# A tanh-shrink MLP behind a dynamic convolution: one f tile in halves, and the first x tile loaded body first

## The chip, the cores and the metric

The kernel runs on one core of a Trainium2 chip. Times are device microseconds (us) of one execution. A profile is one further execution, recorded with all engines: PE is the matmul engine (TensorE) and PEld its weight loads, DVE is VectorE, ACT is ScalarE, POOL is GpSimd, SP is SyncE, which issues most of the DMAs. "L257" is line 257 of the kernel before.

## The reference

`x` is 8 x 4096 x 192 in float32, `weight_gen` 8 x 4096 x 8 heads x 7 taps, `moe_w_in` 192 x 2048, `moe_w_out` 2048 x 192. A softmax over the taps gives each position and head seven weights; they weigh the current row and the six rows ahead of it (zeros before the start of a batch). The result goes through a two-layer MLP whose activation is `h - tanh(h)`:

```python
w = exp(weight_gen - max); w = w / (sum(w) + 1e-9)
x_unf = x_pad[:, idx]                      # 7 rows for each position, K = 7
conv = einsum('bshk,bskhg->bshg', w, x_unf)   # 32768 x 192
h = conv @ w_in                            # 32768 x 2048
out = (h - tanh(h)) @ w_out                # 32768 x 192
```

## The kernel before, in words

The 32,768 tokens are cut into 32 superblocks of 1,024 tokens, numbered n; a partition holds J = 8 consecutive tokens. Batch starts are every fourth n, where the six halo rows of partition 0 are zeros.

For each n there are three stages, which run for different n at the same time.

Stage one makes the convolution products. `load_x` (L99) brings x with its halo, 14 rows of 192 for each partition, over SP's queue; `load_wg` (L89) brings the tap weights. `softmax_exp` (L132) is one exponential on ACT, `softmax_norm` (L142) a sum and a reciprocal on DVE. `products` (L169) multiplies x by the weights, one operation for each of the seven taps k, all on POOL except for n = 0 and 1, where DVE takes some (`on_vector`). For n = 0 DVE has taps 3, 4, 5 and 6 and POOL taps 0, 1 and 2. For n above 2 a DMA on POOL's queue adds the odd products to the even ones.

Stage two is `conv` (L217): PE transposes the products and sums them in PSUM by 64x64 matmuls against an identity, and ACT copies the sums to `convT` (L244). From n = 2 on, superblock n + 1 is transposed inside superblock n, after the f tiles 12 and 13: 104 matmuls into two PSUM tiles called `pc`, the first for chunks 0 and 1, the second for chunk 2.

Stage three is the MLP. `gemm1(n, f)` (L252) makes one of 16 f tiles: six matmuls of 512 columns into a PSUM tile `ph` of 128 x 1024 float32 [...], a tanh on ACT into `th` (L267), and the subtraction on DVE into the bf16 tile `gt` (L269). `gemm2` (L276) makes one token block of the second matmul from the 16 `gt` tiles of superblock n - 1, 32 matmuls into `obank`, and ACT copies the result out (L307).

`ph` and `pc` share one rotation of three PSUM buffers (tag "ph", `psum_h` with bufs = 3), so a matmul that opens a new tile waits until the tile three earlier has been read by all its readers. The order of work is written out by hand (`manual_schedule`): each engine runs its instructions in program order. In a superblock n > 1, step p = 0 to 7 is: f tile 2p, f tile 2p + 1, one `gemm2`. At p = 6 the two `conv` calls come after it, and then the sum and reciprocal for superblock n + 3. So around the transposes the tiles take the buffers in this order: f tile 12 the first, f tile 13 the second, `pc` of chunks 0 and 1 the third, `pc` of chunk 2 the first, f tile 14 the second, f tile 15 the third, f tiles 0 and 1 of the next superblock the first and the second.

At the start, SP issues in this order: tap weights of 0, then x of 0 (zero rows, row block 0, partitions 1 to 15, partitions 16 to 127: L117, L121, L107), tap weights of 1, x of 1. POOL first waits for the normalised weights of n = 0 and then issues three DMAs for the first part of `w_in` (columns below `FA` = 8 x 128, L358), and makes its three products; behind tap 2 it issues the rest of `w_in`. Each part of `w_in` is loaded to the lower 64 partitions and then copied to the upper 64 (L369): the first copy is issued on ACT's queue, the second on SP's.

Of the kernel before, what the change touches and what calls it, by code (L numbers as in the profile page):

```python
# [11 lines left out]
ACT = mybir.ActivationFunctionType  # L12
# [4 lines left out]
def kernel(  # L17
# [8 lines left out]
    nc = tc.nc  # L26

    B, S, D = x.shape
    H, K = weight_gen.shape[2], weight_gen.shape[3]
    G = D // H  # L30
    F = moe_w_in.shape[1]
    P = nc.NUM_PARTITIONS
    R = P // 2
    HALO = K - 1

    J = 8
    TOK = P * J
# [3 lines left out]
    NTOT = B * NSB  # L41
    NFT = F // P
    NC = D // R
    GC = G // NC
# [31 lines left out]
    last_act = {}  # L76
    g1_act = {}
    last_sub = {}
    last_wsm = {}

    def order(inst, other, reason):
        tc.add_manual_dep(
            inst.ins,
            other.ins.name,
            mybir.DependencyInfo(mybir.DependencyClass.Sync, mybir.DependencyReason.DATA),
            reason=reason,
        )

    def load_wg(n):  # L89
        b, s = divmod(n, NSB)  # L90
        s0 = s * TOK
        wg_t = wgpool.tile([P, J, H, K], FP32, name="wg_t")
        nc.sync.dma_start(  # L93
            out=wg_t[:],
            in_=weight_gen[b, s0 : s0 + TOK].rearrange("(p j) h k -> p j h k", p=P),
        )
        wg_of[n] = wg_t

    def load_x(n):  # L99
        b, s = divmod(n, NSB)  # L100
        s0 = s * TOK

        x_t = xpool.tile([P, HALO + J, D], FP32, name="x_t")

        def rows(p0, p1):
            win = x[b, s0 + p0 * J - HALO : s0 + p0 * J - HALO + 1]
            nc.sync.dma_start(  # L107
                out=x_t[p0:p1, :, :],
                in_=bass.AP(
                    tensor=win.tensor,  # L110
                    offset=win.offset,
                    ap=[[J * D, p1 - p0], [D, HALO + J], [1, D]],
                ),
            )

        if s == 0:
            nc.sync.dma_start(  # L117
                out=x_t[0:1, 0:HALO, :],
                in_=zero[:].rearrange("o (h d) -> o h d", h=1).to_broadcast([1, HALO, D]),
            )  # L120
            nc.sync.dma_start(  # L121
                out=x_t[0:1, HALO : HALO + J, :],
                in_=x[b, 0:J].rearrange("(p j) d -> p j d", p=1),
            )

            rows(1, 16)
            rows(16, P)
        else:
            rows(0, P)
        x_of[n] = x_t  # L130

    def softmax_exp(n):  # L132
        wg_t = wg_of.pop(n)
        e_t = wgpool.tile([P, J, H, K], FP32, name="e_t")
        nc.scalar.activation(  # L135
            out=e_t[:].rearrange("p j h k -> p (j h k)"),
            in_=wg_t[:].rearrange("p j h k -> p (j h k)"),
            func=ACT.Exp,
        )
        e_of[n] = e_t  # L140
# [21 lines left out]
    def scale(eng, wsm, e_t, zr):  # L162
        return eng.tensor_mul(  # L163
            wsm.rearrange("p j h k -> p (j h) k"),
            e_t[:].rearrange("p j h k -> p (j h) k"),
            zr.rearrange("p (n o) -> p n o", o=1).to_broadcast([P, J * H, K]),
        )

    def products(n, on_vector=(), sums=None, hooks={}, behind=None):  # L169
        x_t = x_of.pop(n)  # L170
        wsm, wsm_v, e_t, zr = wsm_of.pop(n)
        if e_t is not None:
            first = scale(nc.gpsimd, wsm[:], e_t, zr[:])
            if behind is not None:


                order(first, behind, "pace")
        in_pairs = n not in PLAIN

        even = ppool.tile([P, NPAIR, NC, J, H, GC], BF16, name="even")  # L180
        odd = ppool.tile([P, NPAIR, NC, J, H, GC], BF16, name="odd")
        last = ppool.tile([P, NC, J, H, GC], BF16, name="last")
        dst = {}
        for i in range(NPAIR):
            dst[2 * i] = even[:, i]
            dst[2 * i + 1] = odd[:, i]
        dst[K - 1] = last[:]
        if -1 in hooks:
            hooks[-1]()
        for k in range(K):  # L190
            eng, w = (nc.vector, wsm_v) if k in on_vector else (nc.gpsimd, wsm[:])
            eng.tensor_mul(  # L192
                dst[k].rearrange("p c j h g -> p j h c g"),
                x_t[:, k : k + J, :].rearrange("p j (h c g) -> p j h c g", h=H, c=NC),
                w[:, :, :, k : k + 1]
                .rearrange("p j h (k o) -> p j h k o", o=1)
                .to_broadcast([P, J, H, NC, GC]),
            )
            if k == K - 2 and in_pairs:

                nc.gpsimd.dma_start(  # L201
                    out=even[:].rearrange("p i c j h g -> p (i c j h g)")[:, 0:ACC],
                    in_=odd[:].rearrange("p i c j h g -> p (i c j h g)")[:, 0:ACC],
                    accum_op=mybir.AluOpType.add,
                    max_dma_last_dim=4096,
                )
            if k in hooks:
                hooks[k]()
        if in_pairs:
            groups = [even[:, i] for i in range(NPAIR)] + [last[:]]  # L210
            prods_of[n] = [
                groups + ([odd[:, NPAIR - 1]] if c == NC - 1 else []) for c in range(NC)
            ]
        else:
            prods_of[n] = [[dst[k] for k in (sums or range(K))]] * NC
# [33 lines left out]
        if parts[-1][-1] == NC - 1:  # L249
            prods_of.pop(n)  # L250

    def gemm1(n, f):  # L252
        convT = conv_of[n]
        ph = psum_h.tile([P, 2, HT], FP32, name="ph", tag="ph")
        for c in range(NC):
            for r in range(2):
                nc.tensor.matmul(  # L257
                    ph[:, r, :],
                    lhsT=w_in[r * R : (r + 1) * R, c, f * P : (f + 1) * P],
                    rhs=convT[r * R : (r + 1) * R, c, :],  # L260
                    start=(c == 0),
                    stop=(c == NC - 1),
                )
        th = tpool.tile([P, TOK], FP32, name="th")
        ph_f = ph[:].rearrange("p r t -> p (r t)")
        g1_act[0] = last_act.get(0)
        last_act[0] = nc.scalar.activation(out=th[:], in_=ph_f, func=ACT.Tanh)  # L267
        gt = gpool.tile([P, TOK], BF16, name=f"gt{f}", tag=f"gt{f}")
        last_sub[0] = nc.vector.tensor_sub(gt[:], ph_f, th[:])  # L269
        g_of.setdefault(n, []).append(gt)  # L270

    LAST = (NTOT - 1) * J
# [76 lines left out]
    def load_w_out():  # L349
        nc.gpsimd.dma_start(out=w_out[:], in_=moe_w_out.rearrange("(c p) e -> p c e", c=NFT))  # L350

    FA = 8 * P

    def load_w_in(f0, f1):

        for c in range(NC):
            src = moe_w_in[c * GC : c * GC + 1, f0:f1]
            dma = nc.gpsimd.dma_start(  # L358
                out=w_in[0:R, c, f0:f1],
                in_=bass.AP(  # L360
                    tensor=src.tensor, offset=src.offset, ap=[[G * F, H], [F, GC], [1, f1 - f0]]
                ),
            )
            if f0 == 0:

                order(dma, last_wsm[0], "order of the loads")

    def copy_w_in(f0, f1, eng):
        eng.dma_start(out=w_in[R:P, :, f0:f1], in_=w_in[0:R, :, f0:f1])  # L369

    def rest_of_w_in():
        load_w_in(FA, F)

# [4 lines left out]
    load_wg(1)  # L378
    load_x(1)
    load_w_in(0, FA)  # L380
    products(
        0,
        on_vector=(3, 4, 5, 6),
        sums=(3, 0, 4, 5, 1, 6, 2),
        hooks={2: rest_of_w_in},
    )
    softmax_exp(1)
# [1 line left out]
    load_wg(2)  # L389
    copy_w_in(0, FA, nc.scalar)  # L390
    copy_w_in(FA, F, nc.sync)
    products(1, on_vector=(0, 1), hooks={4: load_w_out})
    conv(0, (0, 1), (2,))
    load_x(2)
    for n in range(NTOT):
        if n + 3 < NTOT:
            load_wg(n + 3)
            load_x(n + 3)
        for p in range(J):
            gemm1(n, 2 * p)  # L400
            gemm1(n, 2 * p + 1)
            if n == 0 and p == 1:
                softmax_exp(2)
            if p == 5 and n + 3 < NTOT:
                softmax_exp(n + 3)
            if n >= 1:
                gemm2((n - 1) * J + p)
            if p == 0 and 1 <= n < NTOT - 2:
                products(n + 2, behind=last_sub[0] if n > 1 else None)
            if n + 1 < NTOT:  # L410
                if p == (6 if n > 0 else 7):
                    conv(n + 1, (0, 1))
                if p == (6 if n > 1 else 7):
                    conv(n + 1, (2,))
            if n == 0 and p == 2:
                softmax_norm(2)
                products(2)
            if p == 6 and n + 3 < NTOT:
                softmax_norm(n + 3)
# [33 lines left out]
```

The softmax here doesn't subtract the row's maximum and nothing guards it: scores larger than these inputs give would overflow.

## Time and profile before

| | |
|---|---|
| time, median of 3 runs | 770.32 us (770.04 to 771.87) |
| the profiled execution's own time | 770.86 us |
| its span (first to last instruction) | 768.7 us |
| busy: PE, DVE, ACT, POOL | 96%, 85%, 83%, 90% |
| granted TensorE clock | 1.00 |
| one tanh of 128x1024 (L267) | 1,022 ns, 512 of them |
| one subtraction of 128x1024 (L269) | 1,219 ns, 512 of them |
| one product on POOL (L192) | 2,903 ns |

The profile page has the busy share of each engine, the span in slices, the chain of work that ended last, and groups of instructions by line with the idle time ahead of them and what ended it. The trace behind it can be asked for a timeline of a stretch: the start, the length, engine, line, what is written and read, and how often. Equal instructions that follow each other are merged ("x2"); the length is then that of the whole group. A bracket at the end is the idle time of that engine ahead of the group, and what ended it.

### The profile page before, as it was taken

How to read it: one execution, taken by the hardware profiler on the slowest of the kernel's cores; microseconds unless marked ns; L12 is line 12 of the kernel's file. 1: busy time of each engine (PE TensorE's matmuls, PEld its weight loads, DVE VectorE, ACT ScalarE, POOL GpSimd, SP SyncE). 2: the span in 40 equal slices, each digit the busy share in tenths (PEclk: the TensorE clock that was granted, in tenths of full speed). 3: DMA queues.
4: the chain of work that ended last, by engine and by line, in shares of the span. 5: the costliest groups of instructions: out<-in, count | busy, mean ns of one | idle time of the engine just before them, and what ended most of it. 6: DMA issues, size and time to landing. Idle time of an engine off the chain costs nothing.

```text
span 768.7 us, 32330 instructions
## 1 busy us (share of the span) xinstructions
PE 736.7 (96%) x14784; PEld 583.1 (76%) x14784; DVE 652.9 (85%) x595; ACT 640.8 (83%) x865; POOL 695.2 (90%) x290
## 2 busy tenths in 40 slices
PE   2799999999999999999999999999999999999997
PEld 2377787777777777788777777777778777787777
DVE  5987888888898888889888888888888988888883
ACT  1777878888888888888888888888888888888883
POOL 5999999999999999999999999999999999999100
PEclk9999999999999999999999999999999999999999
DMA  7823776555677555577655557765556765542412
GB/s 209 184 81 87 182 181 150 118 145 147 169 182 174 131 129 148 150 180 182 164 123 133 150 160 182 180 128 137 143 150 172 182 181 115 125 142 72 98 43 84
DMA packets 25847, 111.37 MB, mean 145 GB/s; under 512 B 4800, under 2 KB 9456, under 8 KB 21624
## 3 DMA queue, kind: packets, MB, share of 16 engines
q1 hardware_dynamic: 14688, 76.95, 29.9%
q0 software_dynamic: 10816, 31.99, 25.8%
q8 instruction: 115, 1.88, 1.0%
q10 hardware_dynamic: 208, 0.39, 0.2%
q14 instruction: 20, 0.16, 0.1%
HBM read 54.49 MB, written 25.17 MB: 104 GB/s over the span
## 4 chain that ended last, share of the span: by engine, by line
PE 93%; DVE 2%; issue 1%; POOL 1%; DMA 1%; ACT 1%; SPq 0%; POOLq 0%
PE ph L257 43%; PE obank L289 43%; PE pc L233 6%; DVE gt L269 2%; PE po L323 1%; DMA x_t<-in_x_dram 1%; POOL even L192 1%; ACT th L267 0%; ACT convT L244 0%; POOL odd L192 0%; DVE zr L151 0%; DVE zsum L145 0%; SPq L117 0%; SPq L93 0%; SPq L121 0%
## 5 line engine op out<-in xcount | busy, mean ns | idle before, releaser
L269 DVE TENSOR_TENSOR gt<-ph,th 128x1024 bf16<-128x1024 f32 x512 | 602.8, 1219 | 93.3 <-ACT th L267 92.7
L267 ACT ACTIVATE th<-ph 128x1024 f32<-128x1024 f32 x512 | 497.2, 1022 | 65.7 <-PE ph L257 64.9
L257 PE MATMUL ph<-convT,w_in 64*128 64x512 bf16 x3072 | 382.1, 378 | 7.5 <-DVE gt L269 5.0
L289 PEld LDWEIGHTS <-gt 64*128 64x128 bf16 x7936 | 345.1, 94 | 53.4 <-issue 2.5
L289 PE MATMUL obank<-w_out,gt 64*128 64x192 bf16 x7936 | 374.6, 243 | 2.9 <-issue 2.1
L192 POOL TENSOR_TENSOR even<-x_t,wsm 128x1536 bf16<-128x1536 f32 x94 | 272.8, 2903 | 3.9 <-DMA x_t<-in_x_dram 1.6
L192 POOL TENSOR_TENSOR odd<-x_t,wsm 128x1536 bf16<-128x1536 f32 x93 | 269.9, 2903 | 0.0
L257 PEld LDWEIGHTS <-w_in 64*128 64x128 bf16 x3072 | 180.1, 94 | 108.4 <-issue 11.8
L192 POOL TENSOR_TENSOR last<-x_t,wsm 128x1536 bf16<-128x1536 f32 x31 | 103.4, 3336 | 0.0
L307 ACT ACTIVATE out_sb<-obank 128x192 f32<-128x192 f32 x248 | 81.9, 330 | 10.5 <-PE obank L289 4.6
L244 ACT ACTIVATE convT<-pc 128x1024 bf16<-128x1024 f32 x64 | 48.9, 808 | 31.6 <-PE pc L233 31.5
L233 PE MATMUL pc<-ident,even 64*128 64x64 bf16 x2304 | 47.9, 192 | 2.9 <-POOL even L192 1.5
L233 PEld LDWEIGHTS <-even 64*128 64x128 bf16 x2304 | 42.7, 96 | 4.1 <-issue 2.2
L201 POOL DMA_DIRECT2D even<-odd x29 | 34.9, 1205 | 9.1 <-POOL odd L192 9.1
L163 POOL TENSOR_TENSOR wsm<-e_t,zr 128x448 f32<-128x448 f32 x30 | 41.7, 1390 | 0.0
L233 PE MATMUL pc<-ident,odd 64*128 64x64 bf16 x448 | 15.5, 198 | 13.1 <-DVE odd L192 12.8
L135 ACT ACTIVATE e_t<-wg_t 128x448 f32<-128x448 f32 x32 | 18.5, 578 | 8.2 <-DMA wg_t<-in_weight_gen_dram 8.2
L233 PE MATMUL pc<-ident,last 64*128 64x64 bf16 x768 | 23.3, 192 | 1.8 <-issue 1.7
L145 DVE TENSOR_REDUCE zsum<-e_t 128x64 f32<-128x448 f32 x32 | 19.5, 609 | 2.9 <-ACT e_t L135 2.9
L233 PEld LDWEIGHTS <-odd 64*128 64x128 bf16 x448 | 11.3, 100 | 13.6 <-DVE odd L192 12.9
L151 DVE RECIPROCAL zr<-zsum 128x64 f32<-128x64 f32 x30 | 16.6, 553 | 3.0
L233 PEld LDWEIGHTS <-last 64*128 64x128 bf16 x768 | 17.0, 96 | 2.2 <-issue 1.8
(20 smaller groups left out, 48.7 us busy)
## 6 DMA issues: line engine op xcount, KB each, us to landing
x_t<-in_x_dram SPq DMA_DIRECT2D x24, 1344.0 KB
even<-odd POOLq DMA_DIRECT2D x29, 1024.0 KB, 8.8
out_dram<-out_sb SPq DMA_DIRECT2D x31, 768.0 KB
x_t<-in_x_dram SPq DMA_DIRECT2D x8, 1176.0 KB
wg_t<-in_weight_gen_dram SPq DMA_DIRECT2D x32, 224.0 KB
x_t<-in_x_dram SPq DMA_DIRECT2D x8, 157.5 KB
w_in<-in_moe_w_in_dram POOLq DMA_DIRECT2D x6, 128.0 KB, 7.5
w_out<-in_moe_w_out_dram POOLq DMA_DIRECT2D x1, 768.0 KB, 10.8
```

What stands on the lines that cost most here:

```text
L135: nc.scalar.activation(out=e_t[:].rearrange("p j h k -> p (j h k)"), in_=wg_t[:].rearrange("p j h k -> p (j h k)"), func=ACT.Exp,)
L145: nc.vector.reduce_sum(out=zsum[:], in_=e_t[:].rearrange("p j h k -> p (j h) k"), axis=AX.X)
L163: return eng.tensor_mul(wsm.rearrange("p j h k -> p (j h) k"), e_t[:].rearrange("p j h k -> p (j h) k"), zr.rearrange("p (n o) -> p n o", ...
L192: eng.tensor_mul(dst[k].rearrange("p c j h g -> p j h c g"), x_t[:, k : k + J, :].rearrange("p j (h c g) -> p j h c g", h=H, c=NC), w[:, : ...
L201: nc.gpsimd.dma_start(out=even[:].rearrange("p i c j h g -> p (i c j h g)")[:, 0:ACC], in_=odd[:].rearrange("p i c j h g -> p (i c j h g)" ...
L233: nc.tensor.matmul(pc[:, r, col : col + R], lhsT=prods[c][gi][r * R : (r + 1) * R, c, 2 * j : 2 * j + 2].rearrange("p j h g -> p (j h g)") ...
L244: nc.scalar.activation(out=convT[:, c0 : c0 + nch, :].rearrange("p c (j r t) -> p r (c j) t", r=2, t=R), in_=pc[:, :, 0 : nch * JH * R].re ...
L257: nc.tensor.matmul(ph[:, r, :], lhsT=w_in[r * R : (r + 1) * R, c, f * P : (f + 1) * P], rhs=convT[r * R : (r + 1) * R, c, :], start=(c == ...
L267: last_act[0] = nc.scalar.activation(out=th[:], in_=ph_f, func=ACT.Tanh)
L269: last_sub[0] = nc.vector.tensor_sub(gt[:], ph_f, th[:])
L289: mm = nc.tensor.matmul(po[:, 0:D], lhsT=g_of[n][f][r * R : (r + 1) * R, col : col + P], rhs=w_out[r * R : (r + 1) * R, f, :], start=(r == ...
L307: last_act[0] = nc.scalar.activation(out=out_sb[:, j, :], in_=po[:, 0:D], func=ACT.Copy)
```

## The change

First, `gemm1` gets a number of parts. For f tile 12 (p = 6) of the superblocks 1 to 30 it is 2: tanh of columns 0 to 511, subtraction of these columns, tanh of columns 512 to 1023, subtraction of these. All other tiles stay whole.

Second, for n = 0 the x tile is loaded as the eight own rows of all 128 partitions, then the six halo rows of partitions 16 to 127, of 1 to 15, and the zeros of partition 0. For the other batch starts the same transfers remain as before.

Third, beside these: the taps of n = 0 are taken in the order 6, 0, 3, 1, 4, 5, 2 (DVE has 6, 3, 4, 5 in this order, POOL 0, 1, 2), the sums in PSUM follow in the order 6, 3, 0, 4, 5, 1, 2, and `FA` is 7 x 128, so that the first part of `w_in` is 896 columns wide and the second 1,152.

```diff
-        def rows(p0, p1):
-            win = x[b, s0 + p0 * J - HALO : s0 + p0 * J - HALO + 1]
+        def rows(p0, p1, r0=0, r1=HALO + J):
+            win = x[b, s0 + p0 * J - HALO + r0 : s0 + p0 * J - HALO + r0 + 1]
             nc.sync.dma_start(
-                out=x_t[p0:p1, :, :],
+                out=x_t[p0:p1, r0:r1, :],
...
-                    ap=[[J * D, p1 - p0], [D, HALO + J], [1, D]],
+                    ap=[[J * D, p1 - p0], [D, r1 - r0], [1, D]],
...
+        if n == 0:
+            rows(0, P, HALO, HALO + J)
+            rows(16, P, 0, HALO)
+            rows(1, 16, 0, HALO)
+            no_halo()
+        elif s == 0:
+            no_halo()
+            rows(0, 1, HALO, HALO + J)
             rows(1, 16)
             rows(16, P)
...
-        for k in range(K):
+        for k in order_of or range(K):
...
-    def gemm1(n, f):
+    def gemm1(n, f, parts=1):
...
-        last_act[0] = nc.scalar.activation(out=th[:], in_=ph_f, func=ACT.Tanh)
         gt = gpool.tile([P, TOK], BF16, name=f"gt{f}", tag=f"gt{f}")
-        last_sub[0] = nc.vector.tensor_sub(gt[:], ph_f, th[:])
+
+        for q in range(parts):
+            t0, t1 = q * TOK // parts, (q + 1) * TOK // parts
+            last_act[0] = nc.scalar.activation(
+                out=th[:, t0:t1], in_=ph_f[:, t0:t1], func=ACT.Tanh
+            )
+            last_sub[0] = nc.vector.tensor_sub(gt[:, t0:t1], ph_f[:, t0:t1], th[:, t0:t1])
...
-    FA = 8 * P
+    FA = 7 * P
...
-        on_vector=(3, 4, 5, 6),
-        sums=(3, 0, 4, 5, 1, 6, 2),
+        on_vector=(6, 3, 4, 5),
+        order_of=(6, 0, 3, 1, 4, 5, 2),
+        sums=(6, 3, 0, 4, 5, 1, 2),
...
-            gemm1(n, 2 * p)
+            gemm1(n, 2 * p, 2 if p == 6 and 0 < n < NTOT - 1 else 1)
             gemm1(n, 2 * p + 1)
```

More of the change, by code (lines that the diff above doesn't have):

```diff
@@ L111, in rows, with no_halo @@
                     offset=win.offset,
-                    ap=[[J * D, p1 - p0], [D, HALO + J], [1, D]],
+                    ap=[[J * D, p1 - p0], [D, r1 - r0], [1, D]],
                 ),
             )
-        if s == 0:
+        def no_halo():
             nc.sync.dma_start(
@@ L120, in load_x @@
             )
[L121 to L124, printed above, removed]
+        if n == 0:
[6 more added lines that the diff above has]
+            rows(0, 1, HALO, HALO + J)
             rows(1, 16)
@@ L167, in scale, with products @@
         )
-    def products(n, on_vector=(), sums=None, hooks={}, behind=None):
+    def products(n, on_vector=(), order_of=None, sums=None, hooks={}, behind=None):
         x_t = x_of.pop(n)
@@ L360, in load_w_in @@
                 in_=bass.AP(
-                    tensor=src.tensor, offset=src.offset, ap=[[G * F, H], [F, GC], [1, f1 - f0]]
+                    tensor=src.tensor,
+                    offset=src.offset,
+                    ap=[[G * F, H], [F, GC], [1, f1 - f0]],
                 ),
```

## The prediction

> **What bounds the kernel now.** I read the page first: shares of busy time and the chain of work that ended last.
>
> ```profile
> PE 736.7 (96%) x14784; PEld 583.1 (76%) x14784; DVE 652.9 (85%) x595; ACT 640.8 (83%) x865; POOL 695.2 (90%) x290
> ...
> PE 93%; DVE 2%; issue 1%; POOL 1%; DMA 1%; ACT 1%; SPq 0%; POOLq 0%
> ```
>
> PE carries the chain from superblock to superblock. So I read PE, ACT and DVE in the timeline of one superblock around the transposes, where the split tile stands.
>
> ```profile
> 338.59 1.48 PE L257 MATMUL ph<-convT,w_in 64*128 64x512 bf16 x12
> 339.88 1.50 PE L289 MATMUL obank<-w_out,gt 64*128 64x192 bf16 x32
> 341.21 0.88 PE L233 MATMUL pc<-ident,even 64*128 64x64 bf16 x48
> ...
> 342.60 0.48 PE L233 MATMUL pc<-ident,odd 64*128 64x64 bf16 x8
> 342.92 1.45 PE L257 MATMUL ph<-convT,w_in 64*128 64x512 bf16 x11
> ```
>
> ```profile
> 339.45 1.94 ACT L267 ACTIVATE th<-ph 128x1024 f32<-128x1024 f32 x2
> 341.42 0.33 ACT L307 ACTIVATE out_sb<-obank 128x192 f32<-128x192 f32 x1
> 342.36 1.51 ACT L244 ACTIVATE convT<-pc 128x1024 bf16<-128x1024 f32 x2 [0.60 <-PE pc L233]
> 343.78 1.02 ACT L267 ACTIVATE th<-ph 128x1024 f32<-128x1024 f32 x1
> ```
>
> ```profile
> 340.51 2.36 DVE L269 TENSOR_TENSOR gt<-ph,th 128x1024 bf16<-128x1024 f32 x2 [0.26 <-ACT th L267]
> 342.78 0.61 DVE L145 TENSOR_REDUCE zsum<-e_t 128x64 f32<-128x448 f32 x1
> ```
>
> The subtractions of tiles 12 and 13 end at 340.51 + 2.36 = 342.87; tile 14, which takes tile 13's PSUM buffer, begins at 342.92, .05 later: that is the price of a hand-over from DVE to PE. The transposes run at about .029 a pair, so PE could have begun tile 14 at about 342.74. It stands .18. In PE's timeline the 29 superblocks 2 to 30 look so in 24 cases; in five (transposes from 112.08, 159.15, 182.12, 227.70 and 431.73) PE stands longer inside the transposes ("issue"), and tile 14 begins 1.68, .29, .36, .31 and .30 after the subtraction, with nothing to gain there.
>
> At the start the bound is the x tile:
>
> ```profile
> 10.28 1.75 DVE L192 TENSOR_TENSOR odd<-x_t,obank 128x1536 bf16<-128x1536 f32 x1 [3.77 <-DMA x_t<-in_x_dram]
> 10.32 2.90 POOL L192 TENSOR_TENSOR even<-x_t,wsm 128x1536 bf16<-128x1536 f32 x1 [1.57 <-DMA x_t<-in_x_dram]
> 13.19 2.90 POOL L192 TENSOR_TENSOR odd<-x_t,wsm 128x1536 bf16<-128x1536 f32 x1
> 16.05 2.89 POOL L192 TENSOR_TENSOR even<-x_t,wsm 128x1536 bf16<-128x1536 f32 x1
> ```
>
> POOL's three products end at 18.94, later than DVE's four (17.03). The first f tile begins at 20.73 and its second half's weights at 20.85, when the copy of `w_in` has landed; after that superblock 0 goes at DVE's pace.
>
> [...] x of 1 (10,752 B packets) starts at 9.44 when x of 0 is through.
>
> **The split tile.** One tanh becomes two, one subtraction two. ACT pays for 512 columns .593 (the 128x512 copy of L244 has this mean), DVE .69. If these overlapped, tile 13 would be free earlier. But the changed program as built has a wait that the diff doesn't show: in all 30 superblocks the second half's tanh waits for DVE's semaphore, at the count that the first half's subtraction brings it to. Both read the one tile `ph`, and the dependency is kept for the tile[...]. So the halves go in turn, and behind the waiting tanh, in ACT's order, stand tile 13's tanh, the copy of `obank` and the copies to `convT`. From the same start, with hand-overs from ACT to DVE of .03 (tanh end 340.48 to 340.51) and from DVE to ACT of .04 (not shown where it decides; between .02 and .10):
>
> - tanh a 339.45 to 340.04; subtraction a 340.07 to 340.76
> - tanh b 340.80 to 341.39; subtraction b 341.42 to 342.11
> - tanh 13 begins .10 before tanh b ends (two tanhs take 1.94, one 1.02): 341.29 to 342.31
> - subtraction 13: 342.34 to 343.56; tile 14 at 343.61 instead of 342.92
>
> That is .69 later. The second `pc` tile needs tile 12's buffer at 342.16 instead of 342.14: nothing. The copy of `obank` moves to 342.21, the first copy to `convT` to 342.44 to 343.46; tile 15 wants that buffer at 343.61 + .65 = 344.26: hidden, by .8. Tile 14's tanh follows PE again, and all that comes later shifts along. POOL, at 22.64 a superblock, no longer paces anything.
>
> Sum: 24 x .69 = 16.6. In the five others the standing counts against it: .69 - .24, - .31, - .26, - .25 is .45, .38, .43, .44, and 0 in the first: 1.7. In superblock 1 only tile 15 has to wait, .1. Together 18.4. Bounds for one superblock: if halves cost exact halves (.51, .61) the lag is .69 - .22 = .47; with a hand-over of .10 and .05 more in the halves it is .80. So 13 to 21.
>
> **The start.** SP issued the large part of x of 0 at about 2.86, behind the zeros (.83), the row block (.37) and 15 partitions; now its body is second, at about 1.2, and follows the tap weights without a gap, whose packets end at 2.9, where x began at 3.43. The bytes are the same (128 x 6,144 + 127 x 4,608 = 127 x 10,752 + 6,144). So the halo lands .6 to 1.5 earlier, near 9.1; POOL cannot begin before its three `w_in` DMAs are issued (6.84 + 1.92 = 8.76). I take 1.2 for POOL. DVE begins tap 6 at about 6.6 and ends its four at 14.1; PE still waits for POOL's tap 2. x of 1 and tap weights of 1 on SP move forward with it. The copy of `w_in` is the next one late: its load shares the engines with x of 1, which ends .7 earlier, and 12.5% fewer bytes save .3 in the load and .2 in the copy: 1.1 earlier. I take 1.1 for the first f tile.
>
> FA has a price: tile 7, not 8, is the first to need the second copy, which is larger by an eighth. It landed at 30.21 before; POOL issues its load 1.2 earlier, larger pieces cost .5, so 29.5, while tile 7's turn is 29.53 - 1.1 = 28.4. PE stands 1.1. What hides it: DVE then has the subtractions of tiles 5 and 6 and, as its timeline shows, sum and reciprocal between them (30.53 to 31.64); tile 7's subtraction is due at 31.63 and its tanh ends at 29.5 + .87 + 1.02 = 31.39. Cover .2; gone if the copy lands after 29.7. So the start gives -1.1, between -1.6 and +.8. [...]
>
> **Sum.** 768.7 + 18.4 - 1.1 = 786.0 span. The profiled execution's own time was 2.2 above its span, so 788.2 for one like it; the median of the runs is 1.62 above that span, so 787.6.
>
> **Rivals.**
> - The added wait doesn't decide. If tanh b could run beside subtraction a, tanh 13 would end at 341.45 and tile 13 be free at 342.70. Tile 14 would begin .17 earlier, but tile 1 of the next superblock then waits for tile 14's subtraction, whose tanh stands behind the `convT` copies on ACT (343.28 + .59): that leaves .08. 24 x .08 = 1.9, with the start 3.0: 767.3. It decides if tanh b starts before about 340.11; against it stands the wait at the count of subtraction a, which ends near 340.76.
> - Part of the loss replaces standing that is there already. PE stands for "issue" in .9% of the chain after 45 us, 6.5 us. If [...] these vanish, 781.1. Against it: most of them lie inside the transposes, ahead of the wait.
> - The start costs. If the halo lands no earlier and tile 7 stands past its cover, +.8 instead of -1.1: 789.5. It lies within the first case.
>
> **How the numbers follow.** The serial halves at full price .84, partly covered .09, not deciding .07. About .3% (2.3 us) is what a measurement here tells from no change. Faster .05, same .02, slower .93. The range is 782.5 to 791.5: the bounds of the lag (13 to 21) with the start's; it leaves out the last rival, half of the second and the outermost of the first.
>
> **What would show it.** Right: 30 pairs of 512-column tanhs with a subtraction between them, tile 14 about .7 later behind the transposes, DVE's release of PE near .87 in each superblock, a superblock of 23.3 instead of 22.63. The start: POOL's first product near 9.1, the first f tile near 19.6. Wrong: tanh b beginning within .5 of tanh a, or superblocks of 22.6; for the start, tile 7's subtraction late.

## The result, and the profile after

| | before | after |
|---|---|---|
| median of 4 runs each | 770.49 us | 788.38 us (787.99 to 788.74) |
| ratio, 95% interval | | 1.0229 (1.0211 to 1.0247) |
| span of the profiled execution | 768.7 us | 785.9 us |
| first f tile begins | 20.73 us | 19.18 us |
| first transposing matmul in superblock 2 | 88.47 us | 87.24 us |
| the same in superblock 30 | 727.09 us | 743.52 us |
| one regular superblock | 22.630 us | 23.416 us |
| from superblock 30's transposes to the end | 41.64 us | 42.43 us |

The kernel is 17.9 us slower; 787.6 was predicted. "A regular superblock" here and below is the distance between the first transposing matmuls of two neighbouring superblocks, where PE doesn't stand for "issue" between them. The span is 17.2 longer: -1.23 up to superblock 2, +17.66 from there to superblock 30, +.79 from there to the end. The page of the kernel after shows, against 93% PE and 2% DVE before, a chain that now runs through DVE and ACT for a quarter of the time:

```profile
PE 740.3 (94%) x14784; PEld 581.0 (74%) x14784; DVE 657.6 (84%) x625; ACT 641.0 (82%) x895; POOL 696.2 (89%) x290
...
PE 70%; DVE 17%; ACT 8%; issue 3%; POOL 1%; DMA 1%; SPq 0%; POOLq 0%
```

The 30 more instructions on ACT and on DVE (895 against 865, 625 against 595) hardly change the busy time. What they change stands in the timeline of the same place as in the prediction, the transposes of one superblock; first PE, then ACT, then DVE, of the kernel after:

```profile
345.42 0.88 PE L238 MATMUL pc<-ident,even 64*128 64x64 bf16 x48
346.12 0.41 PE L238 MATMUL pc<-ident,last 64*128 64x64 bf16 x16
346.47 0.53 PE L238 MATMUL pc<-ident,even 64*128 64x64 bf16 x24
...
346.93 0.30 PE L238 MATMUL pc<-ident,odd 64*128 64x64 bf16 x8
347.92 1.47 PE L262 MATMUL ph<-convT,w_in 64*128 64x512 bf16 x12 [0.69 <-DVE gt L279]
```

```profile
343.67 0.60 ACT L276 ACTIVATE th<-ph 128x512 f32<-128x512 f32 x1
345.09 1.51 ACT L276 ACTIVATE th<-ph 128x512 f32<-128x512 f32 x2 [0.83 <-DVE gt L279]
346.49 0.34 ACT L317 ACTIVATE out_sb<-obank 128x192 f32<-128x192 f32 x1
346.70 1.54 ACT L249 ACTIVATE convT<-pc 128x1024 bf16<-128x1024 f32 x2
348.84 1.94 ACT L276 ACTIVATE th<-ph 128x1024 f32<-128x1024 f32 x2 [0.60 <-PE ph L262]
```

```profile
343.25 1.81 DVE L279 TENSOR_TENSOR gt<-ph,th 128x1024 bf16<-128x1024 f32 x2
345.72 0.69 DVE L279 TENSOR_TENSOR gt<-ph,th 128x512 bf16<-128x512 f32 x1 [0.66 <-ACT th L276]
346.64 1.23 DVE L279 TENSOR_TENSOR gt<-ph,th 128x1024 bf16<-128x1024 f32 x1 [0.22 <-ACT th L276]
```

The brackets carry the reading. ACT idles .83 before the second half's tanh, released by DVE's subtraction; DVE idles .66 before its second half, released by ACT. The halves go in strict turn: 343.67 tanh a, about 344.37 subtraction a (the second of the two in the merged entry), 345.09 tanh b, 345.72 subtraction b. Tile 13's tanh is the second in the entry at 345.09, its subtraction ends at 346.64 + 1.23 = 347.87, and .05 later PE begins tile 14. From the first transposing matmul to tile 14 it was 341.21 to 342.92, 1.71; now it is 345.42 to 347.92, 2.50. The difference, .79, is the whole change of a regular superblock (.786).

The start, DVE then POOL, of the kernel after:

```profile
6.43 1.75 DVE L197 TENSOR_TENSOR last<-x_t,obank 128x1536 bf16<-128x1536 f32 x1
8.55 1.75 DVE L197 TENSOR_TENSOR odd<-x_t,obank 128x1536 bf16<-128x1536 f32 x1 [0.37 <-DMA x_t<-zero]
```

```profile
6.84 1.92 POOL L368 DMA_DIRECT2D w_in<-in_moe_w_in_dram  x3 [5.53 <-DVE wsm L168]
8.75 2.94 POOL L197 TENSOR_TENSOR even<-x_t,wsm 128x1536 bf16<-128x1536 f32 x1
```

DVE's first product is now tap 6, which reads own rows only; it begins at 6.43. Before, DVE's first was tap 3, which waited for x until 10.28. POOL's first product is at 8.75 instead of 10.32, and no DMA holds it any more: it follows the issue of the `w_in` transfers, which ends at 8.76. The last piece of x, its zero rows, landed at 8.43 (before, the last piece landed at 10.16).

### The profile page after: what moved, and what is told of

The parts are those of the page before. It is cut to its first block, busy times and chain, and to the rows that moved or that the text cites. A ratio compares the mean times of both kernels' runs of the same rounds, so it can differ in the third digit from the quotient of the medians.

```text
span 785.9 us, 32390 instructions
## 1 busy us (share of the span) xinstructions
PE 740.3 (94%) x14784; PEld 581.0 (74%) x14784; DVE 657.6 (84%) x625; ACT 641.0 (82%) x895; POOL 696.2 (89%) x290
## 4 chain that ended last, share of the span: by engine, by line
PE 70%; DVE 17%; ACT 8%; issue 3%; POOL 1%; DMA 1%; SPq 0%; POOLq 0%
PE ph L262 35%; PE obank L299 32%; DVE gt L279 17%; ACT th L276 8%; PE po L333 1%; POOL even L197 1%; DMA x_t<-zero 1%; PE pc L238 1%; ACT convT L249 0%; POOL odd L197 0%; SPq L107 0%; DVE zr L156 0%; DVE zsum L150 0%; SPq L93 0%; DVE out_sb L345 0%
## 5 line engine op out<-in xcount | busy, mean ns | idle before, releaser
L279 DVE TENSOR_TENSOR gt<-ph,th 128x1024 bf16<-128x1024 f32 (+1 forms) x542 | 607.5, 1160 | 108.8 <-ACT th L276 108.5
L276 ACT ACTIVATE th<-ph 128x1024 f32<-128x1024 f32 (+1 forms) x542 | 502.2, 975 | 106.3 <-PE ph L262 81.0
L262 PEld LDWEIGHTS <-w_in 64*128 64x128 bf16 x3072 | 176.8, 94 | 130.5 <-issue 34.4
L238 PEld LDWEIGHTS <-even 64*128 64x128 bf16 x2304 | 44.4, 96 | 5.9 <-POOL even L197 2.9
L168 POOL TENSOR_TENSOR wsm<-e_t,zr 128x448 f32<-128x448 f32 x30 | 31.8, 1060 | 15.0 <-DVE gt L279 15.0
```

What stands on the lines that cost most here:

```text
L168: return eng.tensor_mul(wsm.rearrange("p j h k -> p (j h) k"), e_t[:].rearrange("p j h k -> p (j h) k"), zr.rearrange("p (n o) -> p n o", ...
L238: nc.tensor.matmul(pc[:, r, col : col + R], lhsT=prods[c][gi][r * R : (r + 1) * R, c, 2 * j : 2 * j + 2].rearrange("p j h g -> p (j h g)") ...
L262: nc.tensor.matmul(ph[:, r, :], lhsT=w_in[r * R : (r + 1) * R, c, f * P : (f + 1) * P], rhs=convT[r * R : (r + 1) * R, c, :], start=(c == ...
L276: last_act[0] = nc.scalar.activation(out=th[:, t0:t1], in_=ph_f[:, t0:t1], func=ACT.Tanh)
L279: last_sub[0] = nc.vector.tensor_sub(gt[:, t0:t1], ph_f[:, t0:t1], th[:, t0:t1])
```

## The experiments

Each experiment was timed in alternation with the kernel before on the same chip, where the kernel before had a median of 770.3 to 770.6. E1 to E4 shared one chip, E5 and E7 to E9 a second, E6 and E10 a third, so differences are taken against the kernel before beside them. "Standing" in the table is what the stretch from superblock 2's transposes to superblock 30's takes beyond 28 regular superblocks: for before 727.09 - 88.47 - 28 x 22.630 = 4.98.

| kernel | us | ratio to before (95%) | regular superblock | standing |
|---|---|---|---|---|
| before | 770.49 | | 22.630 | 4.98 |
| after | 788.38 | 1.0229 (1.0211–1.0247) | 23.416 | .63 |
| E1 start only | 769.22 | .9984 (.9975–.9992) | 22.630 | 4.58 |
| E2 split only | 789.86 | 1.0252 (1.0237–1.0268) | 23.416 | .69 |
| E3 both tanhs first | 771.30 | 1.0015 (1.0005–1.0025) | 22.755 | 3.38 |
| E4 pair of tiles | 768.71 | .9978 (.9968–.9987) | 22.605 | 4.96 |
| E5 split tile 8 | 778.49 | 1.0106 (1.0091–1.0121) | 23.033 | 2.17 |
| E6 FA = 8 x 128 | 769.00 | .9983 (.9976–.9989) | 22.63 | 5.02 |
| E7 pair, later copy | 767.84 | .9970 (.9959–.9981) | 22.494 | 7.70 |
| E8 later copy alone | 768.72 | .9983 (.9975–.9992) | 22.630 | 4.44 |
| E9 old loads | 770.18 | .9997 (.9988–1.0005) | 22.63 | 4.59 |
| E10 old taps | 769.01 | .9979 (.9970–.9987) | 22.63 | 4.59 |

**E1 and E2: each part alone.** E1 takes the split out of the changed kernel, E2 puts the split alone into the kernel before.

```diff
 E1, against after
-            gemm1(n, 2 * p, 2 if p == 6 and 0 < n < NTOT - 1 else 1)
+            gemm1(n, 2 * p)
 E2, against before
...
-            gemm1(n, 2 * p)
+            gemm1(n, 2 * p, 2 if p == 6 and 0 < n < NTOT - 1 else 1)
```

> All f tiles whole, the new start kept. Theory (the wait between the two halves makes the whole loss, the start gives back 1.2 us): 769.2 us, within 768.6 to 770.0, and a superblock of 22.63 us again. Rival (the start is at fault, or the new order of the taps disturbs what follows): a good part of the 18 us stays, above 775.

> The kernel before with nothing but tile 12 in halves. Theory: the changed kernel's time plus the 1.2 us of the start, 789.6 us, superblocks of 23.42 us. Rival (the start is at fault): near 771. A second rival, that the two parts feed each other, would give a sum of the two single effects that isn't that of both: more than 1 us off.

Measured 769.22 and 789.86. Against the runs of before beside them (770.57) the start gives -1.35 and the split +19.29, together +17.9, which is what both together cost. The sum shows no sign that the parts disturb each other, and the slow-down is the split's alone.

**E3: the order, with the same four operations.** Is it the wait for subtraction a, or four smaller operations instead of two?

```diff
-        for q in range(parts):
-            t0, t1 = q * TOK // parts, (q + 1) * TOK // parts
+        cut = [(q * TOK // parts, (q + 1) * TOK // parts) for q in range(parts)]
+        for t0, t1 in cut:
             last_act[0] = nc.scalar.activation(
...
+        for t0, t1 in cut:
             last_sub[0] = nc.vector.tensor_sub(gt[:, t0:t1], ph_f[:, t0:t1], th[:, t0:t1])
```

> Still two tanhs and two subtractions for tile 12, but both tanhs stand ahead of both subtractions, so no tanh waits for VectorE; the first subtraction now waits for the second tanh. Theory (the loss is the tanh's wait and what is queued behind it): tile 13's subtraction ends about .14 us later than with whole tiles, 24 times, so 2 to 3.5 us over the kernel with the new start alone: 771 to 773 us. Rival (the loss is the fixed cost of four instructions instead of two, or of passing a semaphore more often): most of the .785 us a superblock stays, 782 or more.

Measured 771.30. ACT and DVE of E3 at a superblock's transposes, which begin there at 591.23:

```profile
589.48 2.00 ACT L276 ACTIVATE th<-ph 128x512 f32<-128x512 f32 x3
```

```profile
590.60 2.42 DVE L280 TENSOR_TENSOR gt<-ph,th 128x512 bf16<-128x512 f32 x3 [0.32 <-ACT th L276]
```

The three tanhs (a, b, tile 13) run without a break in 2.00, the three subtractions in 2.42; in the kernel before two tanhs took 1.94 and two subtractions 2.36. The halves as such lengthen a superblock by .125 (22.755 against 22.630); the turn-taking is the other .66 of the .786.

**E4: the dependency's unit.** Every third buffer of the rotation becomes two tiles of 512 columns each instead of one of 1,024. Tile 12 gets such a pair in each superblock, and so do four other f tiles (0, 3, 6, 9), whose tanh and subtraction then go in halves too, and the second `pc`. The order on each engine is that of the changed kernel: tanh a, subtraction a, tanh b, subtraction b.

```diff
+    def psum_tile(name):
+        at = count[0] % 3
+        count[0] += 1
+        if at == 2:
+            two = [psum_h.tile([P, HT], FP32, name=name, tag=f"half{r}", bufs=1) for r in range(2)]
+            return [t[:] for t in two], None
+        t = psum_h.tile([P, 2, HT], FP32, name=name, tag="ph", bufs=2)
+        return [t[:, r, :] for r in range(2)], t
...
-        ph = psum_h.tile([P, 2, HT], FP32, name="ph", tag="ph")
+        ph, whole = psum_tile("ph")
...
```

> [...] these are all handled in halves, in the order of the changed kernel (tanh a, subtraction a, tanh b, subtraction b), and no half waits for the other. Theory (the dependency that is kept for the one PSUM tile is the cause): the loss is gone though there are more halves, 768 to 770 us, and at most .08 us a superblock under the start alone. Rival (halves cost by themselves, in this order): above 780, since some 170 tiles are split instead of 30.

Measured 768.71: with five f tiles in halves instead of one, the loss is gone. ACT of E4 (transposes at 566.17) and DVE:

```profile
564.40 2.00 ACT L298 ACTIVATE th<-ph 128x512 f32<-128x512 f32 x3
...
568.77 1.04 ACT L298 ACTIVATE th<-ph 128x1024 f32<-128x1024 f32 x1
```

```profile
564.00 3.66 DVE L299 TENSOR_TENSOR gt<-ph,th 128x1024 bf16<-128x1024 f32 x4
```

ACT makes both halves and tile 13 in one run of 2.00, while DVE makes four subtractions without a break, so tanh b runs beside subtraction a: the single records have tanh b from 564.89 to 565.49 and subtraction a from 565.13 to 565.81, neither longer (.60 and .68) than in the kernel after, where they go in turn. In these .36 us (565.13 to 565.49) they read the two halves of what was one buffer. The wait in the changed kernel comes from the kernel's tiles and their dependencies, not from the engines: it is kept for the whole tile of 1,024 columns. The tile `th`, which tanh b writes while subtraction a reads its other half, is no rival: in E4 `th` is still one tile, and so is `gt`, and tanh b doesn't wait.

The split does here what one would hope of it: from the transposes to tile 14 it is 1.54 (566.17 to 567.71) instead of 1.71. But the superblock is only .025 shorter. PE of E4 shows where the rest went; below it are PE at the same tiles and ACT at tile 14 of E1, whose transposes begin at 566.79:

```profile
567.71 1.51 PE L282 MATMUL ph<-convT,w_in 64*128 64x512 bf16 x12
...
570.36 1.58 PE L282 MATMUL ph<-convT,w_in 64*128 64x512 bf16 x12
```

```profile
571.11 1.48 PE L262 MATMUL ph<-convT,w_in 64*128 64x512 bf16 x12
```

```profile
569.36 1.02 ACT L276 ACTIVATE th<-ph 128x1024 f32<-128x1024 f32 x1
```

The line at 570.36 holds the next superblock's tiles 0 and 1: 1.58, where the same group takes 1.48 in E1 (tiles 14 and 15, at 567.71, lose another .04). Tile 1 waits for tile 14's subtraction, and tile 14's tanh isn't earlier: at 568.77 it is 2.60 after the transposes began, against 2.57 in E1, since on ACT it stands behind the copies to `convT`. Some .07 of this is E4's own: its second `pc` is copied in two pieces, and the copies take 1.58 instead of 1.51.

**E7 and E8: the second gate.** The copy of the second `pc` to `convT` goes behind tile 14's tanh on ACT, in E7 on top of E4, in E8 on whole tiles.

```diff
             gemm1(n, 2 * p)
+            while held:
+                held.pop(0)()
             gemm1(n, 2 * p + 1)
...
-                    conv(n + 1, (2,))
+                    conv(n + 1, (2,), later=held if n > 1 else None)
```

(With `later`, `conv` puts its copy into the list `held` instead of making it at once.)

> [...] the copy of the second transposed tile stands behind tile 14's tanh on ScalarE instead of ahead of it. Theory (with free halves the wait at tile 14 is gone, but tile 1 of the next superblock then waits for tile 14's subtraction, late by the copies): the gain appears only with both, .13 us a superblock under whole tiles: 22.50 us, 765.3 to 766.8. Rival (the pairs have brought all there is, .025 a superblock): 768 to 769.

> Whole tiles, the new start, and the copy of the second transposed tile behind tile 14's tanh. Theory: tile 14 itself still waits for tile 13's subtraction, so there is nothing for its tanh to begin earlier on: 769.2 us as with the new start alone, within .7. Rival (the copies on ScalarE are what holds the superblock): near 766.

ACT of E7 behind transposes that begin at 544.17, and PE at tiles 0 and 1:

```profile
546.58 1.02 ACT L304 ACTIVATE th<-ph 128x1024 f32<-128x1024 f32 x1 [0.23 <-PE ph L288]
547.50 0.66 ACT L270 ACTIVATE convT<-pc 128x256 bf16<-128x256 f32 x2
```

```profile
548.36 1.47 PE L288 MATMUL ph<-convT,w_in 64*128 64x512 bf16 x12
```

Tile 14's tanh now waits for PE (2.41 after the transposes began), and tiles 0 and 1 take 1.47: neither gate is left. The regular superblock is 22.494, as expected; in E8, with the first gate in place, the later copy alone leaves it at 22.630. So the two gates are in series, and nearly all of the gain shows only with both lifted.

The total was missed: 767.84 lies above the expected range and just under the rival's. Against the kernel before beside it E7 gains 2.45 and E1 1.35, so 1.1 more instead of the .136 x 28 = 3.8 that the superblock promises. The superblock of 22.494 speaks against the rival, and the last column of the table has the difference: standing grew from 4.58 to 7.70. E7 is the fastest of all the kernels.

**E5: the split where PE doesn't wait.** Tile 8 instead of tile 12; there is no transpose near, and PE stood for nothing there.

```diff
-            gemm1(n, 2 * p, 2 if p == 6 and 0 < n < NTOT - 1 else 1)
+            gemm1(n, 2 * p, 2 if p == 4 and 0 < n < NTOT - 1 else 1)
```

> The changed kernel with tile 8 (p = 4) in halves instead of tile 12, far from the transposes. Theory (the halves run in turn wherever they stand, and PE pays what the late release exceeds its slack by): tile 8 is released .46 us later, PE's slack for tile 11 is .06, so a superblock is .40 us longer: 12 us less some 2 that replace standing, 778.5 to 781.5. Rival (the wait only costs at the transposes, where three PSUM buffers are tight): 769 to 770.

Measured 778.49, at the lower edge of what was expected, and .403 a superblock. ACT, DVE and PE of E5:

```profile
590.29 1.51 ACT L276 ACTIVATE th<-ph 128x512 f32<-128x512 f32 x2 [0.83 <-DVE gt L279]
```

```profile
590.92 0.69 DVE L279 TENSOR_TENSOR gt<-ph,th 128x512 bf16<-128x512 f32 x1 [0.66 <-ACT th L276]
```

```profile
591.67 0.82 PE L262 MATMUL ph<-convT,w_in 64*128 64x512 bf16 x6 [0.23 <-DVE gt L279]
```

ACT's idle time is the same .83, but another release decides. Tile 11 takes tile 8's buffer, so it waits for the second half's subtraction, which ends at 591.61, .05 before tile 11 begins. From the start of tile 8's matmuls to the end of its subtraction it is 3.62 (median of superblocks 6 to 29), in E1 3.15. PE had .07 in hand there in E1, so .40 of the .47 reaches it, as was expected. Tile 9, whose tanh stands behind the wait, is released .79 later, as tile 13 is at the transposes; but in E1 PE comes to tile 12, which takes tile 9's buffer, .90 after it could have begun, so that lag costs nothing. The wait between the halves is the same at both places, and what it costs depends on the slack of the tiles that are released late.

**E6, E9 and E10: the parts of the start.** All have whole tiles. E6 puts `FA` back to 8 x 128, E9 the loads of x, E10 the order of the taps and of the sums.

```diff
 E6
-    FA = 7 * P
+    FA = 8 * P
 E9
-        if n == 0:
+        if n < 0:
 E10
-        on_vector=(6, 3, 4, 5),
-        order_of=(6, 0, 3, 1, 4, 5, 2),
-        sums=(6, 3, 0, 4, 5, 1, 2),
+        on_vector=(3, 4, 5, 6),
+        sums=(3, 0, 4, 5, 1, 6, 2),
```

> Whole tiles, the new start, but FA = 8 x 128 as in the kernel before. Theory (the load of x makes the gain at the start; FA only moves the copy of w_in by its share of bytes): the first copy lands near 19.5 instead of 19.0 us, so that the first tile's second half waits for it by some .2 us, and tile 8 finds its copy there: 769.4 us, between 769.0 and 769.9. Rival (FA = 7 is needed for the gain): 770.3.

> Whole tiles, new order of the taps and new FA, but x of superblock 0 loaded as in the kernel before. Theory (the gain at the start is the load's): the first product waits for x until 10.2 us again, the first f tile begins near 20.7, 770.5 us. Rival (the order of the taps or the smaller first part of w_in made it): near 769.3.

> Whole tiles, the new loads and FA = 7 x 128, but the taps and the sums in the order of the kernel before. Theory (VectorE's early tap 6 is hidden, since the transposes end with GpSimd's tap 2): VectorE begins at 8.5 instead of 6.5 us and ends all before superblock 0's first subtraction at 21.7, so 769.2 us, within .6. Rival (the early tap carries a part of the gain): 770 or more.

Only E9 gives the gain back: 770.18, an interval that holds 1, and a first f tile at 20.53. POOL of E9 shows the old wait for x, in place of the 8.75 above:

```profile
10.12 2.90 POOL L197 TENSOR_TENSOR even<-x_t,wsm 128x1536 bf16<-128x1536 f32 x1 [1.35 <-DMA x_t<-in_x_dram]
```

E6 and E10 stay at 769.0, with the first f tile at 19.19 in both. In E10 DVE begins its products 2.3 later than in the kernel after, and yet nothing is later behind them:

```profile
8.74 1.75 DVE L197 TENSOR_TENSOR odd<-x_t,obank 128x1536 bf16<-128x1536 f32 x1 [2.23 <-DMA x_t<-zero]
...
21.75 2.50 DVE L279 TENSOR_TENSOR gt<-ph,th 128x1024 bf16<-128x1024 f32 x2 [0.49 <-ACT th L276]
```

The first subtraction begins at 21.75, in the kernel after at 21.73 behind an idle time of 2.33. What DVE wins by taking tap 6 first it spends waiting. The load in two parts is worth 1.2 us (E9 against its runs of before -.11, E1 -1.35); the other two edits are worth nothing that these runs can tell.

## Why the prediction was right, and where its terms were off

**Bound and mechanism: right.** The chain was read as PE's, with an ACT and DVE chain just under it at the transposes; one more serial step there was to become the bound. The turn-taking of the halves is in the trace, E3 and E4 show that it is the cause (the same operations without it cost .125, and with separate tiles nothing), and E2 that the rest of the change has no part in it. The two halves themselves don't need the wait: in E4 ACT and DVE read them side by side for .36 us, and neither operation is longer for it (.60 and .68 against .597 and .686 in turn). The dependency keeps more apart than these reads need.

**The lag: .69 predicted, .786 measured.** The single steps held: a half's tanh takes .597 (.593 was assumed), its subtraction .686 (.69 was an estimate, which also follows from two lengths in the trace before, 1,219 ns for a subtraction of 1,024 columns and 1,748 for a DVE product of 1,536: another 512 less gives 690), the hand-over from DVE to ACT .03 (.04), that from DVE to PE .05 (.05). One step was mis-sized: "subtraction a 340.07", .03 after tanh a. It couldn't begin then, since DVE was still busy with tile 11. The prediction's own line shows it: the entry at 340.51 has an idle time of .26 before it, so DVE was busy until 340.25. With an overlap of .08 between two DVE operations, subtraction a begins at 340.17, .10 late, and everything behind it too. In the kernel after, subtraction 11 runs from 343.25 to about 344.46, past tanh a's end at 344.27. A half that is ready early is no use to an engine that is not yet free.

**The second `pc` tile: "nothing" predicted, .11 measured** (in PE's timeline the first group of the second `pc` begins .35 after the group before it, 346.12 to 346.47, and .24 before, 341.90 to 342.14). It costs nothing more, since PE waits for tile 14 behind it in any case.

**The standing: 1.7 predicted to be absorbed, 4.35 measured.** The sum counted 24 superblocks in full, and five with their standing taken off, 1.7 less than 29 x .69. In fact the standing fell from 4.98 to .63. So the second rival, "part of the loss replaces standing that is there already", was partly true, with two thirds of the 6.5 us it allowed. The two errors cancel: the lag was .096 x 29 = 2.8 too small, the absorbed standing 2.65 too small. Steady state and tail were to cost 18.4 and cost 17.66 + .79 = 18.45. That this sum is right to .1 us is luck, since two of its terms are not. The span came out at 785.9 against 786.0; the .8 between 787.6 and 788.38 arises in the step from the span to the median of the runs, 1.62 in the sum and 2.4 here.

**The start: -1.1 predicted, -1.23 measured at superblock 2's transposes.** The halo was to land "near 9.1" and landed at 8.43; so POOL began at its own limit, the end of its DMA issues, which the prediction had named at 8.76. The first f tile came 1.55 earlier, not 1.1, and .3 of this was gone again by superblock 2. That .3 is not the split's: E1, whose program is the same up to there, has its first f tile at 19.33 and is 1.51 ahead at superblock 2, and the two traces already differ by .31 where tile 12 of superblock 1 begins, at 59.21 and 58.89, ahead of any split. So one trace gives the gain of the start to no better than .3.

The price of `FA` was wrong: the second copy of `w_in` was to land at 29.5 and hold tile 7 for 1.1, hidden by .2. It landed at 27.85, before tile 7's turn, and PE's wait for tile 7 was for DVE:

```profile
28.23 0.82 PE L262 MATMUL ph<-convT,w_in 64*128 64x512 bf16 x6 [0.55 <-DVE gt L279]
```

The larger pieces were to make that load .5 longer, and it took 6.3 us instead of 7.3 from issue to landing. E1, with the same pieces, took 6.0, and E6, with the old ones and the new start, 6.1: no price of the pieces is to be seen, and why the kernel before took longer stays open. Nothing came of this error, as the cover was never needed. In the first part of `w_in` the eighth fewer bytes were to save .3 in the load; it took 8.6 in E1 and in E6 alike.

**The rivals.** "The added wait doesn't decide" is what E4 builds: its 767.3 allowed .08 a superblock, E4 has .025 and 768.71. The prediction named tanh b's start as what decides; the point it gave for it, 340.11, was not tested. The gate behind it, tile 14's tanh behind the `convT` copies, is the one that E7 lifts.

**What stays open: the standing.** Kernels with short superblocks stand more: 22.494 has 7.70, 22.605 4.96, 22.755 3.38, 23.033 2.17, 23.416 .63; those at 22.630 have 4.4 to 5.0. The waits of PE for "issue" from 70 to 745 us, first of the kernel before, then of E7, then of the kernel after:

```profile
PE pc L233 <- issue: 2.8, 5, 1.7
PE obank L289 <- issue: 0.8, 1, 0.8
PE ph L257 <- issue: 0.8, 1, 0.8
```

```profile
PE pc L249 <- issue: 3.9, 4, 1.4
PE obank L325 <- issue: 1.2, 1, 1.2
PE ph L288 <- issue: 1.0, 1, 1.0
```

```profile
PE pc L238 <- issue: 1.8, 3, 1.3
```

(us in total, times, the longest.) So PE stands 4.4 us in this way before, 6.1 in E7 and 1.8 after. In the traces of before, E1, E3, E4, E5, E7 and after there are 33 gaps of over .15 us between 70 and 730 us in which PE stands without waiting for another engine. Each ends 1.2 to 1.6 us after the end of a packet of the instruction queue. Such packets come about every 6.4 us, so by chance one gap in 16 would fall so. And the gaps recur: all twelve traces have one of 1.0 to 1.7 us that ends between 112 and 115 us. The page's line for the queue, of the kernel before as after:

```profile
q8 instruction: 115, 1.88, 1.0%
```

Each of the 115 packets has 16,384 B in the trace. So in these traces the gaps, .2 to 1.7 us each, go together with the packets in time. That PE stands there for its own instructions is the author's estimate from these times alone; no kernel here changed the number of PE's instructions, so it isn't shown, and neither is why a longer superblock stands less.

## What to carry to other kernels

Before cutting an operation into halves so that two engines overlap, look at what the dependency is kept for: here two halves of one tile were handed over in turn, with ACT idle for .83 us between them, and two tiles were not (E4: read side by side for .36). In a serial chain that is worked out from a profile, start each step when its input is there and its engine is free, whichever is later; the start of a line less the idle time in its bracket gives when the engine became free. And a stall that is removed shows only if the next gate behind it, here ACT's copies, has slack (E4 lifts one gate and gains .025 a superblock, E8 the other and gains 0, E7 both and gains .136); ask for both together.

## What the runs showed that was not expected

Time gained in the steady state was mostly lost again to PE's standing: 3.1 of the 3.8 us in E7. And halves as such are nearly free where nothing waits between them: E4 has five f tiles of each superblock in halves, five operations more on DVE and six on ACT, and its superblock is not longer than with whole tiles (22.605 against 22.630).
